# A fixed, searched instruction order for a fused convolution-and-attention kernel, with the convolution kernel's transform moved into attention

## The chip, the cores and the metric

The kernel runs on one core of one Trainium2 chip. The metric is the device time of one execution in microseconds (us), median of several runs. A profile of one execution shows when each engine worked: PE (matmul; PEld its weight loads), DVE (the vector engine), ACT (the scalar engine), POOL (the general engine) and SP (which issues transfers), with the DMA queues beside them.

## The reference

Two results are blended by a gate that comes from the input. S is 2048, D is 640; everything is bfloat16.

```python
g = sigmoid((A_q * gate_w).sum(-1, keepdims=True))
# A: a short causal convolution over k (4 taps), times v, then a long causal
# convolution over all 2048 positions, one kernel per channel
k_shift = sum(k_pad[:, t:t+S, :] * shift_k[:, 3-t] for t in range(4))
kv = k_shift * v
y = irfft(rfft(pad(kv)) * rfft(pad(ssm_k)))[:, :S] + kv * ssm_D
a = q * y                                    # q is A_q
# B: 32 heads of 20, each position sees itself and 7 earlier ones, two apart
qh, kh, vh = split(A_q @ wqkv)
b = softmax(qh . kh[idx] * scale) . vh[idx]  @ wo
out = g * a + (1 - g) * b
```

## The kernel before

**Attention.** Positions are split by parity, so that the distance of two becomes one, and cut into 18 blocks of up to 114 queries and 121 keys. The steps, by the names of their tiles:

- `xpose` (tile `tx` to `xT`): the input comes in eight pieces (`xn`) and is transposed on PE.
- `vproj` (`psv` to `VW`): V for all heads, 18 units of ten matmuls of 320 columns. `VW` holds 21 columns a head: 20 of V and a column of ones, which gives the softmax denominator.
- `qkproj` (`pj` to `stg`): q and k for 128 of 640 columns at a time (`ft` 0 to 4), 30 units of ten matmuls, copied to staging tiles.
- `fragger`: POOL issues a DMA for each head's fragment from `stg` to one of three pairs of buffers `qb`, `kb`. These hold mask rows too, written once by POOL (`masks`).
- `score_gen` (`sc` to `ETall`): per set of four heads, 72 score matmuls and ten exponentials on ACT into a ring of eight buffers (`NET`).
- `pv_gen` (`O` to `oS`): 72 matmuls of 21 columns a set, then on DVE a reciprocal and a multiplication with it into `oS`, in two parts (48 and 24 matmuls).
- `op_tr` and `outproj` (`tr` to `oT`, `op` to `bl`): 90 transposes of the result, then the output projection in 16 tiles, each evacuated by ACT with the factor 1-g.

**Long convolution.** A two-stage transform (stage 1, `s1_unit`: 8 matmuls a unit, 20 units; stage 2, `s2_unit`: 12 matmuls, 22 units) is applied to the convolution kernel (`h_stream`) and to kv (`u_stream`), each in two parts P = 0 and 1. Its results are multiplied with each other on DVE (`products`), where the kernel's transform is needed also with its two halves swapped: `swaps` copies it by eight DMAs of 640 KB from the tiles `SX` and `Hs` to `Hw`. Then come the inverse's first stage (`inverse1`, 320 matmuls, tile `i` to `UC`) and second stage (`final`, 512 small matmuls, `yb`), and in `final` DVE multiplies with q, adds `bl`, and SP stores groups of up to three of the 16 tiles. `conv` computes the four taps on DVE, 42 operations, `conv_v` the product with v.

**What sets the order.** Each step is a generator that asks for an engine, with what it depends on. A planner (class `Plan`) keeps a cost model of the engines, the four PSUM slots and the DMA lanes, and grants at each step the request that could start first, shifted by hand-set priorities (`PRI`). What it decides is a fixed order of instructions on each engine; on the chip each engine works through its list in that order. Three choices in memory matter here: `oS` has a place of its own, the constants `G` of stage 2 and the transform of part 0 (`SX`) lie where the convolution's inputs (`KX`) were, so `load_G` and the stage 1 of the kernel's transform start only after `conv` and `vproj` are done.

```python
def load_G():
    yield Req("S", 1.0, [ev("conv"), ev("grow"), ev("vproj")])
    SX = p0.tile([128, 10240 + 8192], BF, name="SX", tag="KX")
```

Of the kernel before, what the change touches and what calls it, by code (L numbers as in the profile page):

```python
# [39 lines left out]
NET = 8  # L40
# [7 lines left out]
WARM = 8  # L48
BG = 1266.0
# [59 lines left out]
INF = float("inf")  # L109


class Ev:
    __slots__ = ("t", "eng")

    def __init__(self, t=None, eng="X"):
        self.t = t
        self.eng = eng


class Bank:  # L120
    __slots__ = ("free",)

    def __init__(self):
        self.free = Ev(0.0)
# [6 lines left out]
class Req:  # L131


    def __init__(self, engs, cost=0.0, deps=(), take=0, give=(), n=0, move=0.0, pri=None, mode=None, bg=None, mm=0, lean=0.0):
        self.engs, self.cost, self.deps, self.take, self.give, self.n, self.move = engs, cost, deps, take, give, n, move
        self.pri, self.mode, self.bg, self.mm, self.lean = pri, mode, bg, mm, lean


LAT = {("P", "A"): 230.0, ("P", "D"): 230.0, ("A", "P"): 120.0, ("D", "P"): 120.0, ("A", "D"): 100.0, ("D", "A"): 100.0}
SWITCH = 110.0  # L140
LEAN_QK = -248.0
LEAN_V = 87.0
LEAN_H = -137.0
PRI = dict(loads=0, fragger=0, xpose=-9.2, score_gen=-8.6, pv_gen=-5.7, conv=-1.6, conv_v=-24.1, bulk=0, conv_end=0, qkproj=-4.2, vproj=-4.8,
           gate=-0.8, load_G=0, h_slot=0, p2_slot=10.2, u_slot=0, swaps=0, load_T=0, op_tr=4.7, outproj=37.5, load_q=0, products=6.3, final=-18.6,
           h_stream=(-3.7, -4.9), u_stream=(0.9, 2.5), inverse1=(33.7, 30.7))
PAGE = 256
FETCH = 3600.0


class Plan:


    def __init__(self, nslots):
        self.at = dict(P=0.0, A=0.0, D=0.0, G=0.0, S=0.0, Q=0.0)
        self.mode = None
        self.count = 0
        self.page = 0.0
        self.pipe = 2000.0
        self.row = 0.0  # L160
        lane = []
        self.lane = {"S": lane, "Q": lane, "G": []}
        self.slots = [Bank() for _ in range(nslots)]
        self.streams = []
        self.log = []

    def add(self, gen, pri):
        self.streams.append([pri, gen, next(gen)])

    def cost(self, r, e):  # L170
        if r.n:
            return 160.0 + 0.84 * r.n if e == "A" else 140.0 + 1.03 * r.n
        return r.cost[e] if isinstance(r.cost, dict) else r.cost

    def start(self, r, e):
        t = self.at[e]
        if e == "P" and r.mode != self.mode:
            t += SWITCH
        for d in r.deps:
            if d.t is None:  # L180
                return INF
            t = max(t, d.t + LAT.get((d.eng, e), 60.0))
        if r.take:
            free = sorted(s.free.t + 120.0 if s.free.t is not None else INF for s in self.slots)
            t = max(t, free[r.take - 1])
        if r.move and len(self.lane[e]) >= 8:
            t = max(t, self.lane[e][-8])
        if r.bg is not None:
            t = max(t, self.pipe - r.bg)
        return t  # L190

    def best(self, r):
        found = []
        for e in r.engs:
            s = self.start(r, e)
            found.append((s + self.cost(r, e) + (r.lean if e == "A" else 0.0), s, e))
        end, s, e = min(found)
        return s + self.cost(r, e) if s < INF else INF, s, e

    def run(self):  # L200
        while self.streams:
            pick = None
            for k, (pri, gen, r) in enumerate(self.streams):
                end, st, e = self.best(r)
                if st == INF:
                    continue
                p = pri if r.pri is None else r.pri
                key = (st + 120.0 * p, p, k)
                if pick is None or key < pick[0]:
                    pick = (key, k, st, end, e)  # L210
            assert pick is not None, [(s[1].__name__, s[2].engs) for s in self.streams]
            _, k, st, end, e = pick
            pri, gen, r = self.streams[k]
            g = Grant()
            g.eng, g.banks = e, []
            if e == "P":
                c = self.count + 2 * r.mm
                while self.count // PAGE < c // PAGE:
                    into = (self.count // PAGE + 1) * PAGE - self.count
                    x = max(st, self.page) + (end - st) * into / max(1, 2 * r.mm)  # L220
                    late = max(0.0, self.page + FETCH - (st + (end - st) * into / max(1, 2 * r.mm)))
                    st, end = st + late, end + late
                    self.page = st + (end - st) * into / max(1, 2 * r.mm)
                    self.count += into
                    r.mm -= into // 2
                    st = self.page
                    end = max(end, st)
# [724 lines left out]
```

## Time and profile before

| | |
|---|---|
| Median of three runs | 251.53 us (249.74, 251.53, 256.14) |
| The profiled execution | span 246.1 us from its first to its last instruction; its own run time is not listed apart, so what lies around the span is taken as 3.6 us (to the lowest run) to 5.4 us (to the median) |
| PE / DVE / ACT / POOL busy | 215.8 / 185.8 / 168.6 / 68.8 us |
| First score | 42.75 us |
| Last normalization of attention | ends at 139.9 us |
| First inverse stage starts | 197.6 us |
| Second inverse stage starts | 220.9 us |

The busy time of PE in this profile counts a matmul from its start to its modelled end, so two in a row overlap; the distance of two starts is the better price. "Granted clock" is the share of full speed that PE was allowed. A row of the view by stretches reads: stretch, its length, then for PE, PEld, DVE, ACT and POOL the busy us and (x) the number of instructions, then the granted clock, the busy share of the DMA engines, and GB/s. A row of the view by groups reads: line, engine, operation, output<-input, shapes, xcount, then busy us and mean ns of one, then idle time before them and what ended it. A row of the view in order of time reads: start, length, engine, line, operation, [idle before it <- what ended that].

### The profile page before, as it was taken

To read this page: it belongs to the slowest core of one execution; us is meant where nothing else is said; L and a number is where in the kernel's file an instruction comes from. 1 tells how busy PE (TensorE), PEld (TensorE's weight loads), DVE (VectorE), ACT (ScalarE), POOL (GpSimd) and SP (SyncE) were. 2 spreads that over 40 slices of the span, in tenths; PEclk is the share of its full clock that TensorE was granted. 3 is DMA by queue.
4 is the path that set the end of the run, shared out by engine and by line. 5 is a ranking of instruction groups with operands and counts; after the bars stand their busy time and mean duration, and the time that the engine had idled before them with its cause. 6 is when DMAs were issued, how large, how long until landed. Compare 5 with 4: busy or idle time off the path is not lost.

```text
span 246.1 us, 8342 instructions
## 1 busy us (share of the span) xinstructions
PE 215.8 (88%) x3654; PEld 167.2 (68%) x3654; DVE 185.8 (76%) x220; ACT 168.6 (69%) x222; POOL 68.8 (28%) x147
## 2 busy tenths in 40 slices
PE   6799999899796999999999999896979999984590
PEld 2699887776464667565766788785867799983350
DVE  1424499999879999978788899995899993134942
ACT  2143543774478785789889799988375589768871
POOL 6699699106719144619000000000000000000000
PEclk9999999999999799995555599999799999999568
DMA  6999965898994959698910000699939910400754
GB/s 230 305 348 192 177 81 137 148 158 142 180 146 95 150 96 138 122 164 245 257 67 4 3 4 3 151 221 212 218 61 204 268 20 3 109 0 5 179 147 107
DMA packets 59580, 33.83 MB, mean 137 GB/s; under 512 B 49212, under 2 KB 56008, under 8 KB 58904
## 3 DMA queue, kind: packets, MB, share of 16 engines
q1 hardware_dynamic: 55192, 27.08, 55.0%
q0 software_dynamic: 3792, 5.81, 10.5%
q8 instruction: 28, 0.46, 0.9%
q10 hardware_dynamic: 560, 0.42, 0.5%
q14 instruction: 8, 0.07, 0.1%
HBM read 20.01 MB, written 2.62 MB: 92 GB/s over the span
## 4 chain that ended last, share of the span: by engine, by line
PE 49%; DMA 13%; POOL 13%; issue 9%; ACT 9%; DVE 4%; SPq 1%; ACTq 0%; POOLq 0%; DVEq 0%
PE op L854 10%; PE pj L575 9%; PE i L820 7%; PE O L664 6%; DMA Hw<-SX 5%; PE sc L636 5%; ACT ETall L643 4%; PE s L713 4%; DMA kb<-stg 3%; POOL qb L614 3%; DMA mm<-ca_mm 3%; DMA KX<-in_A_k_dram 3%; PE psv L528 2%; POOL kb L427 2%; POOL qb L428 2%
## 5 line engine op out<-in xcount | busy, mean ns | idle before, releaser
L643 ACT ACTIVATE ETall<-sc 121x912 bf16<-121x912 f32 (+1 forms) x80 | 63.4, 855 | 12.5 <-PE sc L636 11.6
L575 PE MATMUL pj<-xT,Wqk 128*128 128x342 bf16 (+1 forms) x300 | 49.0, 314 | 1.0 <-ACT ETall L643 0.6
L575 PEld LDWEIGHTS <-Wqk 128*128 128x128 bf16 x300 | 28.4, 98 | 15.8 <-issue 1.4
L481 DVE TENSOR_TENSOR KX<-KX 128x1760 bf16<-128x1760 bf16 (+1 forms) x24 | 27.6, 1161 | 4.3 <-issue 4.0
L614 POOL DMA_DIRECT2D qb<-stg x36 | 18.1, 505 | 36.8 <-PE sc L636 14.6
L528 PE MATMUL psv<-KX,xT 128*121 128x320 bf16 x180 | 27.3, 300 | 1.0 <-DVE xT L286 1.0
L636 PE MATMUL sc<-qb,kb 31*128 31x114 bf16 x576 | 23.4, 241 | 5.4 <-ACT ETall L643 2.0
L284 ACT CAST UC<-s 128x960 bf16<-128x960 f32 (+2 forms) x25 | 22.3, 971 | 7.9 <-PE s L713 6.7
L854 PE MATMUL op<-wo,oT 128*128 128x512 bf16 (+1 forms) x160 | 25.7, 322 | 0.0
L528 PEld LDWEIGHTS <-xT 128*121 128x121 bf16 x180 | 23.4, 134 | 2.2 <-issue 1.2
L713 PEld LDWEIGHTS <-SX 64*128 64x128 bf16 x512 | 19.5, 96 | 7.8 <-issue 7.0
L636 PEld LDWEIGHTS <-kb 31*128 31x128 bf16 x576 | 13.7, 104 | 15.1 <-issue 9.3
L284 ACT CAST stg<-pj 128x684 bf16<-128x684 f32 (+1 forms) x17 | 12.5, 746 | 14.9 <-PE pj L575 9.2
L284 ACT CAST VW<-psv 121x640 bf16<-121x640 f32 x15 | 10.4, 696 | 17.8 <-PE psv L528 17.8
L854 PEld LDWEIGHTS <-oT 128*128 128x128 bf16 x160 | 17.1, 150 | 7.4 <-issue 2.3
L286 DVE CAST UC<-s 128x1024 bf16<-128x1024 f32 (+1 forms) x17 | 19.5, 1195 | 0.0
L488 DVE TENSOR_TENSOR KX<-KX 128x1760 bf16<-128x1760 bf16 (+1 forms) x18 | 18.8, 1042 | 0.3
L614 POOL DMA_DIRECT2D kb<-stg x36 | 17.9, 505 | 3.4 <-ACT stg L284 2.9
L858 ACT ACTIVATE bl<-op,omg 128x640 bf16<-128x640 f32 x16 | 12.7, 794 | 8.6 <-PE op L854 8.6
L820 PE MATMUL i<-F,Hw 128*128 128x128 bf16 x160 | 18.3, 219 | 0.0
L286 DVE COPY xT<-tx 128x1280 bf16<-128x1280 bf16 x8 | 6.5, 824 | 15.6 <-PE tx L467 15.6
L664 PEld LDWEIGHTS <-ETall 121*128 121x128 bf16 x576 | 16.5, 100 | 2.5 <-issue 1.7
(73 smaller groups left out, 376.4 us busy)
## 6 DMA issues: line engine op xcount, KB each, us to landing
xn<-in_A_q_dram SPq DMA_DIRECT2D x8, 320.0 KB, 8.0
KX<-in_A_k_dram SPq DMA_DIRECT2D x8, 320.0 KB, 11.8
vin<-in_A_v_dram SPq DMA_DIRECT2D x8, 320.0 KB, 7.1
h_lin<-in_A_ssm_k_dram SPq DMA_DIRECT2D x16, 160.0 KB, 4.9
Hw<-SX SPq DMA_DIRECT2D x4, 640.0 KB, 7.8
Hw<-Hs SPq DMA_DIRECT2D x4, 640.0 KB, 11.9
out_dram<-SX SPq DMA_DIRECT2D x20, 120.0 KB, 2.2
kb<-stg POOLq DMA_DIRECT2D x28, 85.1 KB, 3.6
```

Source lines behind the costliest of these rows:

```text
L284: nc.scalar.copy(dst, src)
L286: nc.vector.tensor_copy(dst, src)
L481: eng.tensor_tensor(d, kin[:, n + 3 - j:n + 3 - j + m, :], w.to_broadcast([128, m, QC]), ALU.mult)
L528: nc.tensor.matmul(ps[0:BK, n0 // 320, 0:320], lhsT=xT[:, dt, s0:s0 + BK], rhs=Wv[:, dt, n0:n1], start=(dt == 0), stop=(dt == NDT - 1))
L575: nc.tensor.matmul(ps[:, i, 0:n], lhsT=Wqk[:, dt, w, 128 * ft:128 * ft + 128], rhs=xT[:, dt, s0:s0 + n], start=(dt == 0), stop=(dt == NDT ...
L614: nc.gpsimd.dma_start(dst[r0:r0 + rows, 0:wd], stg[fa - f0:fb - f0, 0:wd])
L636: nc.tensor.matmul(sc[:, hh, BQ * bb:BQ * bb + BQ], lhsT=kb[r:r + DH + NF, BK * b:BK * b + 128], rhs=qb[r:r + DH + NF, BQ * b:BQ * b + BQ] ...
L643: nc.scalar.activation(ETall[0:BK, e, :, 0:BQ * nb], sc[0:BK, :, 0:BQ * nb], ACT.Exp, scale=SCALE)
L664: nc.tensor.matmul(O[:, (b - b0) // 6, c0:c0 + 21], lhsT=ETall[0:BK, e, hh, BQ * bb:BQ * bb + 128], rhs=VW[0:BK, b, 4 * t + h4, :], start= ...
L713: nc.tensor.matmul(ps[:, c, 160 * jj:160 * jj + 160], lhsT=st["G"][rows, j0 + jj, rr, :], rhs=Am[rows, rr].rearrange("p o (q j) l -> p j ( ...
L820: nc.tensor.matmul(d, lhsT=st[(key, P)][:, c, o + il // 4, :, il % 4], rhs=M[:, k, :], start=(k == 0), stop=(k == 1), skip_group_check=True)
L854: nc.tensor.matmul(op[:, n0:n1], lhsT=oT[:, ft].rearrange("p h m a -> p a (h m)")[:, t, :], rhs=wo[:, ft, n0:n1], start=(ft == 0), stop=(f ...
```

## The change

The planner is gone. The order of all requests now stands in the program as a string of 846 letters (`ORDER`), one for each request, with a `-` where the second of two possible engines is taken; a small class (`Steps`) grants them in that order. Apart from that:

- Head: the eight pieces of the input come first on SP, the weights for `ft` 0 and half of V come on ACT's queue after the constants, k comes last row first in three pieces, then its halo. The memsets of `ETall` and `VW` move from POOL to DVE. Twelve warm-up matmuls in place of eight.
- First heads first: `ft` 0 of q and k alternate, and their fragments too; V is projected by halves of the heads (`vproj0`, `vproj1`), the second half during attention.
- `oS` becomes a view of `VW`: the normalized output of a set is written over columns of V that were used up. The tiles `G`, `H0` (transform of part 0, in the place of `xn`) and both `Hw` now have places that come free early, and `h_lin` holds one part at a time.
- The convolution kernel's transform runs from the middle of attention on: all of stage 1, and 16 of the 22 units of stage 2, stand ahead of the last attention matmul. The addition of `ssm_D` moves from POOL to DVE.
- An O matmul takes up to three heads' columns (63, 63, 42, 21); what it writes beyond its own head is overwritten by the next ones. Seven `ETall` buffers in place of eight.
- q is loaded in two halves of eight tiles (`load_q0`, `load_q1`) and multiplied with g on DVE, tile by tile; the second inverse's evacuation is a plain copy, and takes all tiles of a group at once. The groups of the tail are (0,3), (3,3), (6,2), (8,3), (11,3), (14,2).

```diff
-NET = 8
+NET = 7
-WARM = 8
+WARM = 12
+TAIL = [(0, 3), (3, 3), (6, 2), (8, 3), (11, 3), (14, 2)]
...
-class Plan:
+class Steps:
+    def run(self, order):
+        for word in order.split():
+            other = 0
+            for c in word:
+                if c == "-":
+                    other = 1
+                    continue
+                k = STREAMS.index(c)
+                self.grant(k, self.streams[k][1].engs[other])
...
+    G = p0.tile([128, 32, 2, 128], BF, name="G", tag="G")
+    h_lin = p0.tile([128, PL, 2, 64], BF, name="h_lin", tag="HL")
+    xn = p0.tile([128, 8, 2, D], BF, name="xn", tag="H0")
+    VW = p0.tile([128, NB, H, DH + 1], BF, name="VW", tag="VW")
+    oS = VW[:].rearrange("p b h e -> p b (h e)")
...
     def pv_gen():
-  nc.tensor.matmul(O[:, (b - b0) // 6, c0:c0 + 21], lhsT=ETall[0:BK, e, hh, BQ * bb:BQ * bb + 128],
-                   rhs=VW[0:BK, b, 4 * t + h4, :], start=True, stop=True, skip_group_check=True)
+  nh = min(3, 4 - h4)
+  nc.tensor.matmul(O[:, (b - b0) // 6, c0:c0 + 21 * nh], lhsT=ETall[0:BK, e, hh, BQ * bb:BQ * bb + 128],
+                   rhs=VW[0:BK, b, 4 * t + h4:4 * t + h4 + nh, :].rearrange("p h e -> p (h e)"),
+                   start=True, stop=True, skip_group_check=True)
...
-    def load_q():
-        for n, (a, b) in enumerate(((4, 16), (0, 4))):
...
+    def load_q(half):
+        yield Req("N", 0.0, [ev(f"{k}s2{P}") for k in "hu" for P in range(2)] if half else [ev("hs10"), ev("hs11")])
+        q = p0.tile([128, 8, D], BF, name=f"q{half}", tag="G" if half else "HL")
+        for g in range(4):
+            r = yield Req("S", 600.0, move=1400.0)
+            nc.sync.dma_start(q[32 * g:32 * g + 32], ...)
+        for t in range(8):
+            r = yield Req("D", 235.0, [Ev(r.done.src), ev("gate")] if t == 0 else [])
+            nc.vector.tensor_scalar(q[:, t], q[:, t], g_nat[:, 8 * half + t:8 * half + t + 1], None, ALU.mult)
...
     def final():
-  nc.scalar.activation(yb[:, tt, 320 * k:320 * k + 320].rearrange("p (q c) -> p q c", q=2),
-                       pss[k][:, :, 160 * tt:160 * tt + 160], ACT.Copy, scale=g_nat[:, t0 + tt:t0 + tt + 1])
+  copy(r.eng, yb[:, 0:m, 320 * k:320 * k + 320].rearrange("p t (q c) -> p q t c", q=2),
+       pss[k][:, :, 0:160 * m].rearrange("p q (t c) -> p q t c", c=160))
```

In the built order SP's list ends: four loads of `q0`, eight swap copies, four stores of the first group, one load of `q1`, four stores, two loads of `q1`, four stores, the last load of `q1`, twelve stores.

577 lines of the change are left out of this document (250 added, 327 removed).

## The prediction

> **What bounds the kernel now.** I read the page first, then the busy time of each engine in the stretches between the phases, then the groups of instructions, and last the order in time where one phase hands over to the next.
>
> ```profile
> span 246.1 us, 8342 instructions
> PE 215.8 (88%) x3654; PEld 167.2 (68%) x3654; DVE 185.8 (76%) x220; ACT 168.6 (69%) x222; POOL 68.8 (28%) x147
> ...
> 0.00:34.00 34.00, 30.55 (x247) 25.00 (x248) 13.39 (x13) 11.89 (x16) 27.12 (x42) 1.00 1.07 240
> 43.70:138.70 95.00, 87.54 (x1540) 61.24 (x1542) 84.21 (x105) 72.40 (x93) 32.35 (x86) 0.84 0.77 136
> 138.70:183.50 44.80, 38.87 (x811) 33.93 (x809) 40.87 (x41) 35.85 (x42) 0.00 (x0) 0.92 0.56 119
> 183.50:197.60 14.10, 14.10 (x102) 10.40 (x102) 14.10 (x27) 8.52 (x11) 0.00 (x0) 1.00 0.96 214
> 197.60:220.90 23.30, 22.21 (x352) 21.05 (x351) 11.35 (x18) 19.41 (x21) 0.00 (x0) 1.00 0.13 31
> 220.90:246.10 25.20, 13.14 (x542) 8.35 (x541) 12.48 (x12) 16.10 (x35) 0.00 (x0) 0.77 0.41 107
> 112.00:140.00 28.00, 25.88 (x566) 19.20 (x562) 23.50 (x31) 24.24 (x32) 4.34 (x12) 0.50 0.41 107
> ```
>
> No engine is full over the whole span, but one is in each stretch. To 43.7 us PE loads and projects. Attention (43.7 to 138.7; DVE ends its last normalization at 139.9) keeps PE busy for 87.5 of 95.0 us, DVE for 84.2 and ACT for only 72.4. From there to 197.6 DVE sets the pace (54.9 of 58.9 us): copies out of PSUM, then the products. The first inverse stage takes 23.3 us and is full of PE. In the last 25.2 us nothing is full: a chain through all engines and the output stores. The last row is the second fact that matters: from 112 to 140 us the granted clock is 0.50 although PE shows 25.9 of 28.0 us busy.
>
> **Prices.** Busy time over count, so that overlapping starts are taken out.
>
> ```profile
> L643 ACT ACTIVATE ETall<-sc 121x912 bf16<-121x912 f32 x48 | 41.7, 931 | 6.3 <-PE sc L636 5.8
> L643 ACT ACTIVATE ETall<-sc 121x684 bf16<-121x684 f32 x32 | 22.1, 740 | 6.3 <-PE sc L636 5.8
> L284 ACT CAST stg<-pj 128x726 bf16<-128x726 f32 x7 | 5.4, 768 | 5.4 <-PE pj L575 5.4
> L284 ACT CAST VW<-psv 121x640 bf16<-121x640 f32 x15 | 10.4, 696 | 17.8 <-PE psv L528 17.8
> L284 ACT CAST UC<-i 128x1024 bf16<-128x1024 f32 x17 | 16.2, 1020 | 2.7 <-PE i L820 2.2
> L284 ACT CAST UC<-s 128x960 bf16<-128x960 f32 x15 | 13.6, 968 | 5.8 <-PE s L713 4.6 <-ACT UC L284 1.0
> L858 ACT ACTIVATE bl<-op,omg 128x640 bf16<-128x640 f32 x16 | 12.7, 794 | 8.6 <-PE op L854 8.6
> L488 DVE TENSOR_TENSOR KX<-KX 128x1760 bf16<-128x1760 bf16 x15 | 16.1, 1070 | 0.3
> L676 DVE TENSOR_TENSOR oS<-O,rd 114x480 bf16<-114x480 f32 x24 | 15.0, 654 | 0.6
> L673 DVE RECIPROCAL rd<-O 114x48 f32<-114x48 f32 x8 | 3.6, 454 | 2.5 <-PE O L664 2.5
> L286 DVE CAST UC<-s 128x1024 bf16<-128x1024 f32 x12 | 13.8, 1213 | 0.0
> L286 DVE CAST UC<-s 128x960 bf16<-128x960 f32 x5 | 5.7, 1152 | 0.0
> L751 DVE TENSOR_TENSOR Hw<-UC,Hw 128x960 bf16<-128x960 bf16 x20 | 12.9, 647 | 0.0
> L713 PE MATMUL s<-UC,SX 64*128 64x160 bf16 x256 | 12.2, 237 | 4.0 <-DVE oT L286 1.9 <-issue 1.4 <-ACT UC L284 0.5
> L697 PE MATMUL s<-F,h_lin 64*128 64x128 bf16 x160 | 11.8, 291 | 1.0 <-ACT ETall L643 0.8
> ```
>
> **Head of the kernel.** POOL's constants, PE's order and the first conv taps:
>
> ```profile
> 1.84 3.59 PE L438 MATMUL wu<-KX 128*128 128x512 bf16 x8 [1.84 <-DVE KX L435]
> 27.04 1.61 PE L575 MATMUL pj<-xT,Wqk 128*128 128x342 bf16 x10
> 28.49 1.52 PE L528 MATMUL psv<-KX,xT 128*121 128x320 bf16 x10
> 29.84 1.65 PE L575 MATMUL pj<-xT,Wqk 128*128 128x349 bf16 x10
> 42.75 0.67 PE L636 MATMUL sc<-qb,kb 31*128 31x114 bf16 x8
> ...
> 36.23 3.50 POOL L614 DMA_DIRECT2D qb<-stg  x7 [0.19 <-issue]
> 28.27 4.91 DVE L481 TENSOR_TENSOR KX<-KX 128x1760 bf16<-128x1760 bf16 x2 [3.98 <-issue]
> ```
>
> Ten psv matmuls take 29.84-28.49 = 1.35 us, ten pj 28.49-27.04 = 1.45 us. Today PE runs 8 warm-up (3.6), 80 transposes (about 4.5), 140 psv (18.9) and 80 pj (11.6) ahead of the first score: 38.6 us from 1.84 on, and the score starts at 42.75, so 2.3 us are lost. Afterwards it is 12 warm-up (12x0.45 = 5.4), 80 transposes, 90 psv (12.2) and 60 pj (8.7): 30.8 us, first score at 1.84+30.8+2.3 = 34.9. POOL does not hold it up: its first fragment leaves at 36.23 today behind three mask pairs, 16 small instructions, eight halo DMAs and the memsets of ETall and VW; halo DMAs go to SP, the memsets to DVE (which stands idle there), the constant mm is fetched ahead of the weights. POOL is free at about 22 us, the eight fragment DMAs of set 0 take 8x0.5 us, and land near 31. The extra 1.8 us of warm-up lie before the last x block and are counted. But 50 psv (6.8 us) and 20 pj (2.9 us) are only moved behind the first score: the start is 7.9 us earlier and owes PE 9.7.
>
> The conv taps need the first k rows, on SP behind 5.2 MB; at the 240 GB/s of the first row of stretches 5.7 MB arrive at 23.8 us. The two first taps took 4.91 us beside POOL's mask copies; now those are over, and I price all 42 at the L488 row.
>
> **Attention.** It takes in 188 of 256 s2 matmuls of the conv-kernel transform with 16 of 22 copies, all its stage 1, and the 9.7 us. Counted from the built order, from the first score to the last normalization:
> - ACT: 80 exponentials 41.7+22.1 = 63.8; 18 stg copies x0.77 = 13.9; 9 VW x0.69 = 6.2; 8 transform copies, half at 0.95 and half at 0.91, 7.5; the gate 0.7. Sum 92.1 (today 72.4).
> - DVE, from 23.8: 42 taps 35x1.07+7x0.9 = 43.8; normalization 24x0.63 and 16 reciprocals, half of them shorter than the row, 6 together, 21.1; 27 transform copies at about 1.15 = 31; 6 stg 5.2; the four v products 6.2; small ones 1. Sum 108.3, so not before 132.1.
> - PE: 90 psv 12.2, 240 pj 34.8, 188 s2 at 0.048 and 160 s1 at 0.074 at most (its row is mostly from half clock) 20.8, the gate 1.3; scores and O below. Sum at most 98.
>
> ```profile
> 51.98 1.38 PE L664 MATMUL O<-VW,ETall 121*128 121x21 bf16 x48
> 121.41 0.58 PE L636 MATMUL sc<-qb,kb 31*128 31x114 bf16 x16
> ...
> 139.36 0.66 DVE L676 TENSOR_TENSOR oS<-O,rd 114x480 bf16<-114x480 f32 x1
> ```
>
> The O row prices PE's 576 O matmuls at 28 ns with 21 columns, 16.2 us; 576 scores are some 12.6 at full clock, and by the row from 121.41 (16 in 0.58 us) 1.7 times that at half. Widened to as many as 63 columns they stream 63x0.42 ns = 27 ns (0.42 is 1.35 us over ten times 320 columns), under the 28: nothing at full clock. At 0.50 it would be 53 ns, at most 0.9 us more a set on average. That is the bound. I take zero: the row of 0.50 lies where projections had run out, and here they are spread over sets 0 to 5. If the clock falls in sets 6 and 7 alone, PE's 12 us there become some 21 against 16 of ACT: up to 5 us, in the range. [...]
>
> So three engines have 92 to 100 us of work in about 100. ACT is last: 34.9+0.6 to start, 92.1, about 6 us in set 0 in which PE works through 70 pj and 50 psv (17 us) while ACT has 13, and 1.7 for the last O and its normalization: 135.3 if nothing else is lost. The same sum at today's occupancy (72.4/95.0 = 76%) is 34.9+0.6+92.1/0.76+1.7 = 158. Today's ACT was underfed, not obstructed, so I go near the low end: 4.2 us lost, T0 = 139.5, range 135 to 150. Seven ET buffers in place of eight can cost one exponential a set (0 to 7 us); it is inside that range. Attention's end thus stays where it is (139.9); the gain must come behind it.
>
> **Behind attention.** DVE sets the pace: 3 H copies 3.1, 7 u stage-1 copies 8.1, 5 u stage-2 copies 5.4, 5 oT 6.0, gate 0.6, 8 q products (no such row; the 640-element sum at 240.99 below takes 0.49, a quarter of that is the least that I can see, I take 0.3) 2.4, then 28 products x0.645 = 18.1 before the inverse of part 1 may start: 43.7; with 5% loss T0+46. Beside it ACT has 13 copies of 1024, 17 of 960 and 11 op outputs (12.4+15.5+8.7 = 37 us), and PE 324 s2 (15.6), 160 s1 (8 to 12), 90 transposes (5) and 110 op matmuls (15.5; the row of 183.50 has 102 matmuls in 14.10 us): 44 to 48. PE just fits; if not, up to 3 us, in the range.
>
> ```profile
> 170.68 0.66 DVE L751 TENSOR_TENSOR SX<-UC,SX 128x960 bf16<-128x960 bf16 x1 [2.73 <-DMA Hw<-SX]
> ```
>
> Today DVE also waits 2.73 us here for the swaps. They no longer wait for attention's buffers, but still for the last copy (T0+4); 8x0.64 MB at the 214 GB/s of the stretch rows are 24.5 us, T0+30.5, when DVE asks for part 1's at T0+30: covered, 0 to 2 us. Today this way takes 197.6-139.9 = 57.7. Saved: 11.7.
>
> First inverse: 20 copies on ACT alone, 20x0.95+2 = 21.3 against 23.3; the rest of the products (16x0.645 = 10.3) end beside part 1. Saved 2.0. The second inverse starts at 139.5+46+21.3 = 206.8.
>
> **The tail**, where the change costs:
>
> ```profile
> 224.36 1.28 PE L893 MATMUL i<-UC,T 32*32 32x160 bf16 x120 [1.78 <-issue]
> 233.14 5.16 PE L854 MATMUL op<-wo,oT 128*128 128x512 bf16 x20
> ...
> 226.99 16.99 SPq L911 DMA_DIRECT2D out_dram<-SX  x24
> 240.99 0.49 DVE L908 TENSOR_TENSOR SX<-SX,bl 128x640 bf16<-128x640 bf16 x1 [0.28 <-ACT bl L858]
> SX<-in_A_q_dram SPq DMA_DIRECT2D x4, 160.0 KB, 3.4
> ```
>
> ACT's evacuation gets cheaper (two copies of 960 for six scaled ones), but the second half of q is loaded by SP between the stores: the fourth of its DMAs stands behind the stores of the third group, and DVE's q products for tiles 8 to 15 stand ahead of its last three groups. By today's pattern the third group's sum ends 12 us in: two groups with the 1.78 us PE stall, 20 op matmuls (1.41 us each ten at full clock, 2.58 in the row at 233.14), the small group. Then four stores at 0.6 us (4 issues from 241.5 to 244.0), the load 0.5+3.4, eight q products 2.4, three groups 2x2.4+1.7, and today's 4.6 us from the last sum to the end: 12+2.4+3.9+2.4+6.5+4.6 = 31.8 against 25.2. Lost 6.6. Without that wait PE ends near 20, and the tail is 26.5.
>
> **Sum**: 206.8+31.8 = 238.6 against 246.1, that is -0.4 -11.7 -2.0 +6.6 = -7.5. The median of the runs lies 5.4 above the profiled span (251.53), the lowest 3.6; with 5.4: 244.0 us, 3% less. About 2% is what a measurement of this kernel can tell from no change.
>
> **Rivals.**
> 1. The q load does not bite, because DVE reaches it late anyway: 238.6-5.3 = 233.3, so 238.7. Against it: the order in SP's queue is fixed. Chance 0.14.
> 2. The moved transform is paid back in attention: part of its 16 copies (16 us over two engines) prolong it to T0 = 147, span 246.1, 251.5: no change. For it: three engines above 90%. Chance 0.22.
> 3. Slower: ACT, fed in a fixed order by a PE that is itself full, stays at 76% as today. T0 = 158, span 257.1, so 262.5 us. It decides from an occupancy of about 80% down (T0 above 152). Against it: today's low share is largely lack of work. Chance 0.14.
> 4. The clock halves from set 4 on: there PE has 50 pj, 288 scores and O, 80 s1 and 176 s2, some 32 us at full clock and, at the 1.7 of the score row, 55 or more at half, against 39 for ACT, T0 near 156: 260. Against it: sets with 20 to 40 pj kept 1.00 today. Chance 0.04.
>
> The forecast has the remaining 0.46, 239 to 249 by itself. Faster by over 2%: 0.14, most of the forecast and a little of rival 2, 0.56; slower: 3 and most of 4, 0.16; between them 0.28. The range leaves out rivals 3 and 4 and the luckiest ends: 234 to 256.
>
> **What would show it.** First score near 35 us; last normalization near 139.5 (135 and 147 decide between forecast and rival 2) with ACT above 90% between; granted clock 1.00 there (rival 4); first inverse 46 us later; a DVE wait of 5 to 6 us for the q DMA before its last three groups (rival 1: none). I am wrong if the last normalization comes after 150 or that wait is missing.

## The result, and the profile after

The changed kernel takes 275.67 us (median of six runs, 271.55 to 282.04) beside 250.98 us for the kernel before (247.16 to 256.14). The ratio is 1.094, 95% interval 1.080 to 1.108: slower by 9%, where 3% faster was predicted. Below, the time of a kernel is the mean of its undisturbed runs (273.4 us for the changed one, five in two series; 249 to 251 for the one before), since some runs of each kernel are some per cent longer, among them the profiled ones of pe_light, filler, late_part1, quiet_late, late_pe_light and changed_again, whose rows serve for places and shares rather than times. The runs counted for one kernel, two to seven of them, lie up to 4.3 us apart, so a difference of under 3 us between two kernels says little by itself.

First the page of the changed kernel, then its stretches: the phases, and attention cut at the last O of each set (sets 3 and 4 in three pieces).

```profile
span 269.5 us, 8335 instructions
PE 224.4 (83%) x3658; PEld 171.2 (64%) x3658; DVE 178.3 (66%) x227; ACT 176.6 (66%) x217; POOL 54.3 (20%) x126
```

```profile
36.10:64.40 28.30, 25.00 (x277) 17.87 (x278) 18.59 (x19) 17.68 (x24) 9.02 (x26) 0.94 1.06 161
64.40:81.40 17.00, 17.00 (x244) 12.22 (x246) 13.84 (x17) 13.12 (x19) 2.11 (x5) 1.00 1.11 158
81.40:95.80 14.40, 13.64 (x236) 9.26 (x236) 12.02 (x15) 9.83 (x14) 6.56 (x22) 1.00 0.62 117
...
105.40:119.10 13.70, 9.02 (x188) 6.91 (x188) 8.29 (x11) 10.29 (x14) 4.47 (x9) 1.00 1.18 170
119.10:131.40 12.30, 10.94 (x190) 7.35 (x192) 6.58 (x7) 7.82 (x11) 3.50 (x7) 0.80 0.27 74
131.40:145.10 13.70, 12.36 (x214) 8.05 (x212) 9.60 (x11) 9.33 (x13) 3.45 (x7) 0.81 0.19 46
145.10:155.50 10.40, 8.48 (x207) 6.67 (x208) 8.00 (x10) 8.59 (x11) 0.00 (x0) 0.91 0.80 185
155.50:168.00 12.50, 11.45 (x236) 9.39 (x235) 9.39 (x13) 7.55 (x10) 0.00 (x0) 0.66 0.12 21
168.00:217.40 49.40, 43.30 (x658) 35.57 (x653) 41.43 (x61) 36.57 (x43) 0.00 (x0) 0.93 0.51 108
...
236.80:269.50 32.70, 14.70 (x562) 10.14 (x561) 14.75 (x20) 13.52 (x17) 0.00 (x0) 0.79 0.48 122
36.10:168.00 131.90, 117.40 (x1889) 83.56 (x1889) 93.87 (x110) 92.05 (x119) 31.63 (x80) 0.91 0.74 122
```

Against the rows of the prediction the span falls apart like this (us):

| | before | forecast | after |
|---|---|---|---|
| to the first score | 42.8 | 34.9 | 36.1 |
| attention, to the last normalization | 97.2 | 104.6 | 131.7 |
| from there to the first inverse | 57.7 | 46.0 | 49.6 |
| first inverse | 23.3 | 21.3 | 19.4 |
| the rest | 25.2 | 31.8 | 32.7 |
| span | 246.1 | 238.6 | 269.5 |

Four of the five are within 4 us. Attention is off by 27 of the 31 us. ACT is busy there for 92.05 us, as the forecast's sum has it (92.1), yet only 70% of the time. PE is busy for 117.4 where the sum had 98 at most. The rows by set show four kinds of trouble: in set 0 (36.1 to 64.4) PE is busy for 25.0 of 28.3 us; from 64.4 to 95.8 at full clock it has hardly a pause; at 119 us there is a hole (9.02 of 13.7); from 119 on the clock is 0.66 to 0.91.

**What PE's work cost.** Groups of instructions in attention (count | busy us, mean ns | idle us ahead of them), the scores of the kernel before in its own attention, and a piece of the changed kernel in order of time:

```profile
L508 PE MATMUL pj<-xT,Wqk 128*128 128x342 bf16 (+1 forms) x240 | 43.6, 333 | 1.0 <-ACT ETall L586 0.9
L579 PE MATMUL sc<-qb,kb 31*128 31x114 bf16 x576 | 26.9, 225 | 7.1 <-DMA kb<-stg 3.1 <-ACT ETall L586 2.1 <-ACT H L222 0.8
L609 PE MATMUL O<-VW,ETall 121*128 121x63 bf16 (+2 forms) x576 | 19.8, 190 | 1.9 <-ACT ETall L586 0.9 <-issue 0.8 <-DVE SX L224 0.2
```

```profile
L636 PE MATMUL sc<-qb,kb 31*128 31x114 bf16 x576 | 23.4, 241 | 5.4 <-ACT ETall L643 2.0 <-DMA kb<-stg 2.0 <-DVE oS L676 1.1
```

```profile
66.14 0.38 PE L579 MATMUL sc<-qb,kb 31*128 31x114 bf16 x8
66.45 1.57 PE L459 MATMUL psv<-WvT,xT 128*121 128x320 bf16 x10
...
78.39 1.67 PE L508 MATMUL pj<-xT,Wqk 128*128 128x349 bf16 x10
79.99 0.40 PE L641 MATMUL s<-F,h_lin 64*128 64x128 bf16 x8
...
119.14 0.64 PE L641 MATMUL s<-F,h_lin 64*128 64x128 bf16 x8 [2.98 <-DVE h_lin L706]
...
120.19 2.96 PE L508 MATMUL pj<-xT,Wqk 128*128 128x342 bf16 x10
123.09 0.40 PE L641 MATMUL s<-F,h_lin 64*128 64x128 bf16 x8
```

A modelled end overlaps the next start, so I add up distances of starts, without the idle time in brackets. From the first score to the last O, 130.7 us, that gives: scores 24.5 (forecast 12.6), projections 41.8 (34.8), O 18.8 (16.2), psv 13.0 (12.2), the transform 17.6 (20.8), the gate 1.2 (1.3). Together 116.8, and 13.9 us of idle time. The same adding for the kernel before, to its last O, gives 88.6 and 7.2: there are 7.1 us more of projections, 7.1 of psv, 8.9 of transform, 5.1 of scores and O, and 6.7 of idle time. Nearly all that was moved in came on top.

Two causes can be seen. The first is the order. At full clock a unit of 8 scores takes 66.45-66.14 = 0.31 us, and a projection behind scores 79.99-78.39 = 1.60; I had priced 16 scores at 0.35 and the projection at 1.45. My price fits the kernel before where its order puts 16 scores side by side, 46.54-46.20 = 0.34 us:

```profile
46.20 0.40 PE L636 MATMUL sc<-qb,kb 31*128 31x114 bf16 x16
46.54 1.57 PE L528 MATMUL psv<-KX,xT 128*121 128x320 bf16 x10
```

Its group row, 23.4 us for 576 scores, is longer for more than one reason: busy times overlap, and 215 of these scores ran at half clock. The 361 at full clock come to 11.1 us from start to start, 0.49 for 16.

The second cause is the clock: behind the hole at 119 ten projection matmuls take 2.90 us (120.19 to 123.09), at half clock. Sorted by the granted clock, 31 of the changed kernel's 240 projection matmuls ran at half clock, 291 ns each, and 209 at full clock, 157 ns each. So of the 7.0 us by which projections exceed the forecast some 4 are the clock; of the scores' 12 only about 1 is.

**The tail** went as forecast: DVE waits 6.54 us for the fourth of q1's DMAs, which stands behind twelve stores.

```profile
249.77 1.78 SPq L849 DMA_DIRECT2D out_dram<-q  x4
251.59 1.28 SPq L809 DMA_DIRECT2D q<-in_A_q_dram  x1
...
256.28 2.46 DVE L812 TENSOR_SCALAR q<-q,g_nat 128x640 bf16<-128x640 bf16 x8 [6.54 <-DMA q<-in_A_q_dram]
```

### The profile page after: what moved, and what is told of

It reads as the page before. It is cut to its first block, busy times and chain, and to the rows that moved or that the text cites. A ratio compares the mean times of both kernels' runs of the same rounds, so it can differ in the third digit from the quotient of the medians.

```text
span 269.5 us, 8335 instructions
## 1 busy us (share of the span) xinstructions
PE 224.4 (83%) x3658; PEld 171.2 (64%) x3658; DVE 178.3 (66%) x227; ACT 176.6 (66%) x217; POOL 54.3 (20%) x126
## 4 chain that ended last, share of the span: by engine, by line
PE 57%; DMA 15%; ACT 11%; DVE 8%; issue 4%; SPq 2%; POOL 1%; ACTq 0%; DVEq 0%
PE pj L508 16%; PE op L793 8%; PE O L609 6%; PE s L657 6%; ACT UC L222 6%; PE psv L459 5%; PE sc L579 5%; PE i L759 4%; ACT ETall L586 4%; DMA h_lin<-in_A_ssm_k_dram 3%; PE s L641 3%; DMA WvT<-in_B_wqkv_dram 3%; DMA kb<-stg 3%; DMA qb<-stg 3%; DMA q<-in_A_q_dram 2%
## 5 line engine op out<-in xcount | busy, mean ns | idle before, releaser
L508 PE MATMUL pj<-xT,Wqk 128*128 128x342 bf16 (+1 forms) x300 | 52.8, 328 | 1.0 <-ACT ETall L586 0.9
L222 ACT CAST UC<-s 128x960 bf16<-128x960 f32 (+2 forms) x30 | 27.4, 995 | 9.4 <-PE s L657 8.1
L222 ACT CAST stg<-pj 128x684 bf16<-128x684 f32 (+1 forms) x24 | 18.0, 752 | 23.1 <-PE pj L508 16.1
L579 PE MATMUL sc<-qb,kb 31*128 31x114 bf16 x576 | 26.9, 225 | 7.1 <-DMA kb<-stg 3.1
L224 DVE CAST SX<-s 128x1024 bf16<-128x1024 f32 (+1 forms) x20 | 23.3, 1186 | 9.8 <-PE s L641 8.9
L459 PE MATMUL psv<-WvT,xT 128*121 128x320 bf16 x180 | 26.0, 300 | 3.0 <-DMA WvT<-in_B_wqkv_dram 3.0
L579 PEld LDWEIGHTS <-kb 31*128 31x128 bf16 x576 | 15.5, 99 | 18.5 <-issue 10.8
L657 PEld LDWEIGHTS <-G 64*128 64x128 bf16 x512 | 19.8, 99 | 7.4 <-issue 5.6
L609 PE MATMUL O<-VW,ETall 121*128 121x63 bf16 (+2 forms) x576 | 19.8, 190 | 1.9 <-ACT ETall L586 0.9
L222 ACT CAST UC<-i 128x1024 bf16<-128x1024 f32 x20 | 18.4, 1124 | 0.1
L844 DVE TENSOR_TENSOR q<-yb,q 128x1920 bf16<-128x1920 bf16 (+1 forms) x6 | 6.3, 1043 | 18.0 <-ACT yb L222 18.0
```

The lines of the kernel that those rows point to most:

```text
L222: nc.scalar.copy(dst, src)
L224: nc.vector.tensor_copy(dst, src)
L459: nc.tensor.matmul(ps[0:BK, par, 0:320], lhsT=xT[:, dt, s0:s0 + BK], rhs=Wv[:, dt, 320 * hp:320 * hp + 320], start=(dt == 0), stop=(dt == ...
L508: nc.tensor.matmul(ps[:, i, 0:n], lhsT=Wqk[:, dt, w, 128 * ft:128 * ft + 128], rhs=xT[:, dt, s0:s0 + n], start=(dt == 0), stop=(dt == NDT ...
L579: nc.tensor.matmul(sc[:, hh, BQ * bb:BQ * bb + BQ], lhsT=kb[r:r + DH + NF, BK * b:BK * b + 128], rhs=qb[r:r + DH + NF, BQ * b:BQ * b + BQ] ...
L609: nc.tensor.matmul(O[:, (b - b0) // 6, c0:c0 + 21 * nh], lhsT=ETall[0:BK, e, hh, BQ * bb:BQ * bb + 128], rhs=VW[0:BK, b, 4 * t + h4:4 * t ...
```

## The experiments

The leading theory was that PE sets attention's end, because the split order makes its work dearer than its streaming time. The rivals: late data (set 0's fragments, h_lin's second load) with the fall of the clock behind them, and ACT in its fixed order, as in the prediction's third rival. All edits are to the changed kernel, except in prices and before_wide.

### The prices alone

> Not the kernel: matmuls alone, of its shapes, on 128 rows of the input, nothing on ACT or DVE; the output is the input. Sections, each at full clock as far as it goes: projections of ten matmuls with 342 columns back to back; score units of 8 on one half of the row groups only; score units on alternating halves; a lone score unit between projections; two score units, then two projections; O units of 48 with 21 columns and with up to 63; score units between O units of 24. Theory that the split order costs PE: a lone 8 takes 0.28 to 0.35 us and the projection behind it 1.55 to 1.62, so a score and a projection 1.85 to 1.95; side by side two units take 0.35 to 0.40, and the same work in the paired order 1.60 to 1.72 a pair. O of 48: 1.36 to 1.42 us narrow, 1.40 to 1.50 wide. Rival (the prices of the forecast, and the long times in attention are waits that the records don't show): 8 scores 0.18, projection 1.45, O 1.35 in any order.

```profile
30.20 11.76 PE L98 MATMUL ps<-big 128*128 128x342 bf16 x80
41.89 3.49 PE L100 MATMUL ps<-big 31*128 31x114 bf16 x128
45.32 5.97 PE L102 MATMUL ps<-big 128*128 128x342 bf16 x40
...
51.23 1.85 PE L104 MATMUL ps<-big 31*128 31x114 bf16 x128
53.02 5.97 PE L106 MATMUL ps<-big 128*128 128x342 bf16 x40
58.92 0.38 PE L108 MATMUL ps<-big 31*128 31x114 bf16 x8
59.23 1.62 PE L109 MATMUL ps<-big 128*128 128x342 bf16 x10
60.79 0.38 PE L108 MATMUL ps<-big 31*128 31x114 bf16 x8
...
107.11 7.64 PE L118 MATMUL ps<-big 121*128 121x21 bf16 x288
114.59 7.36 PE L120 MATMUL ps<-big 128*128 128x342 bf16 x40
121.79 8.01 PE L122 MATMUL ps<-big 121*128 121x63 bf16 x288
129.65 5.96 PE L124 MATMUL ps<-big 128*128 128x342 bf16 x40
```

From start to start: ten projection matmuls in a row of its own 11.69/8 = 1.46 us. Eight scores on alternating halves of the row groups 1.79/16 = 0.11, always on the same half 3.43/16 = 0.21, alone between projections 0.31, and the projection behind them 1.56. So a score and a projection by turns cost 1.87 where the parts in rows of their own cost 1.57: 0.30 us more, without any other engine. Two and two cost 1.67 each (from 81.34 to 84.68, 3.34 us for two of each). The theory's prices of scores and projections stand, the rival's fall; the O units were cheaper than either had them (1.25 us narrow and 1.31 wide for 48). Why a lone unit costs 0.31 where rows of them cost 0.11 to 0.21 was not shown; the prices by themselves speak against a finely mixed order.

The last rows belong to the clock, below.

### Which engine: less PE work, less ACT work, the units in pairs

```diff
 # pe_light
-for dt in range(NDT):
+for dt in range(NDT if ft == 0 else 3):
 # act_light
-nc.scalar.activation(ETall[0:BK, e, :, 0:BQ * nb], sc[0:BK, :, 0:BQ * nb], ACT.Exp, scale=SCALE)
+nc.scalar.activation(ETall[0:BK, e, :, 0:BQ * nb // 2], sc[0:BK, :, 0:BQ * nb // 2], ACT.Exp, scale=SCALE)
 # pairs (ORDER, one of 23 places)
-eeyyeeyyeejykeef
+yyeeeeyyjykeeeef
```

> Leaves out 2 of the 5 matmul steps of the projections of ft 1 to 4: 96 matmuls of attention, 14 to 15 us of PE, and nothing on ACT, DVE or in the queues. Theory that PE's work bounds attention: its end moves 9 to 15 us earlier. Rival (ACT's order or late data): under 4 us.

> Exponentials over half of their columns (the buffers are filled once ahead): ACT loses some 28 of its 92 us in attention, PE, DVE and the queues nothing. Theory that PE's work bounds attention: its end moves by 2 to 6 us, which are PE's waits for ETall. Rival (ACT's order bounds it): 12 us or more.

> Only the order is changed: the two score units of a block group, which use two row groups of PE each, always stand next to each other (23 pairs joined; runs of 12, 16 and 28 score matmuls in place of 6, 8, 12, 16, 18 and 28; 111 runs on PE in attention in place of 137). Theory that PE bounds attention and that lone score units and switches cost it: a joined pair takes 0.35 to 0.4 us less, the busy time of scores falls from 26.9 to 17 to 20 us, and attention ends 6 to 10 us earlier. Rival (late data and the clock set the end, PE's busy time only fills the waits): scores get shorter, the end moves by under 2 us. Second rival (ACT, fed in bursts, holds PSUM): slower by 1 to 4 us.

pe_light takes 270.3 us: 3 less for 14 us of PE. act_light takes 272.9: nothing for 26 us of ACT.

```profile
38.50:168.60 130.10, 114.14 (x1853) 80.11 (x1854) 90.44 (x106) 66.23 (x118) 31.63 (x80) 0.92 0.69 121
```

ACT is busy for 66.23 us in attention instead of 92.05, and it lasts 130.1 us from first score to last O, where the changed kernel's two profiles have 130.7 and 135.5. That ends the third rival: ACT's order is not the bound. But pe_light missed the leading theory's 9 to 15 us as well. PE's work does set the pace of sets 1 to 3, where PE has hardly a pause: they take 46.2 us in the changed kernel (64.4 to 110.6), 45.0 in act_light, and 42.3 in pe_light, although its clock was 0.95 and 0.87 in two of them. In the same profile its set 0 gave most of that back, at clock 0.75, with 31.6 us in place of 28.3. And pairs, which made scores cheaper as forecast (busy 22.0 us in place of 26.9), was slower by 12: 285.4 us. PE's waits in its attention:

```profile
PE O L609 <- ACT ETall L586: 5.8, 7, 1.1
PE pj L508 <- ACT stg L222: 4.3, 3, 3.2
```

O waits for the last exponential of its group seven times, projections for the place that ACT's copy has to free. Is it ACT's pace? pairs_act_light joins the two edits.

> The paired order together with exponentials over half of their columns, which alone changed nothing. Theory that pairing lost because ACT, given two exponentials at a time, holds PE's four places in PSUM and answers too late: with short exponentials the paired order is no longer slower, 266 to 274 us, and PE's waits for ETall fall from 17 to under 6 us. Rival (pairing loses through late projections and fragments): 280 to 286 us.

278.7 us, between the two forecasts: 6.8 less than pairs, where short exponentials alone gave 0.4. So about half of what pairing lost comes from ACT answering two exponentials at a time too late for PE's four places in PSUM; the other half, 5.8 us over act_light, was not placed. The fine order has a price on PE and hides the way through ACT; in the one paired order that was run, the first did not go without the second.

### Late data: h_lin's second load and set 0

```diff
 # h_once
-yield Req("N", 0.0, [ev("hs10")])
-yield from load_h(1)
 # h_after_set0: only the order, letters "a" behind set 0's "d"
 # quiet_set0: that order, and k's rows 0 to 49 left out
-for q in range(4):
+for q in range(4 if k == 0 else 0):
     nc.sync.dma_start(kin[32 * q:32 * q + 32, 3 + n0:3 + n1, :], ...)
```

> The second load of h_lin (eight DMAs) and its D addition are left out; part 1 of the transform reads part 0's data, so every PE, ACT and DVE step but that addition stays. Theory that PE's own work bounds attention: only the 3.0 us of PE's wait at 119 us go, at most 4 us of the last normalization at 167.8. Rival (late data set attention's end, and the clock drops that follow them): the wait and the half clock from 120 to 145 us both go, 7 to 12 us.

> The first load of h_lin, 1.28 MB, and the first of G start behind set 0's eight fragment DMAs and no longer ahead of them; nothing else is moved. Theory that PE's work bounds attention: set 0's waits of PE (3.1 us for kb) shrink, 2 to 4 us off the 28.3 us of set 0, and as much off the whole. Rival (late data set the pace): 5 to 8 us off set 0. If the pieces of k and not h_lin crowd the queues: under 1 us.

> Leaves out the load of k's rows 0 to 49 (zeros in their place), 2.05 MB, and puts h_lin's first load and the first of G behind set 0's fragment DMAs: next to nothing else is in the queues while set 0's fragments travel. Theory that set 0 is late for its data: it shrinks from 28 to 32 us to 20 to 23 us, no wait for kb or qb stays and the clock is 1.00 from 40 to 48 us; the whole gains 6 to 9 us. Rival (set 0 is full of PE work, 25 us of it): 1 to 3 us.

```profile
117.30:132.80 15.50, 13.25 (x270) 9.47 (x269) 9.80 (x11) 13.78 (x18) 5.26 (x11) 1.00 0.45 125
...
146.10:157.40 11.30, 10.51 (x206) 8.03 (x208) 8.24 (x10) 8.19 (x11) 0.00 (x0) 0.68 0.83 186
157.40:168.00 10.60, 9.55 (x200) 7.49 (x202) 8.30 (x11) 7.60 (x10) 0.00 (x0) 0.70 0.05 9
```

```profile
36.00:60.30 24.30, 22.92 (x275) 17.16 (x276) 18.20 (x19) 17.64 (x24) 6.99 (x14) 1.00 1.07 191
106.50:125.50 19.00, 12.82 (x211) 8.56 (x212) 7.62 (x8) 11.23 (x14) 3.34 (x7) 0.91 0.75 118
```

h_once takes 270.9 us, 2.5 less, as the leading theory has it and far from the rival's 7 to 12. Set 4 falls from 20.8 us (110.6 to 131.4) to 15.5 at clock 1.00 (first row), but the clock falls later instead, to 0.68 and 0.70 in sets 6 and 7. h_after_set0 takes 277.0, 3.6 more, with 31.0 us for set 0: so it was not h_lin's load that crowded set 0. quiet_set0 shrinks set 0 from 28.3 to 24.3 us at clock 1.00, with no wait for a fragment left. The whole is 6.2 us below h_after_set0, whose order it has, and only 2.6 below the changed kernel (270.8): PE then stands still for longer at 112 to 117, 5.1 us in front of h_lin (12.82 busy of 19.0 us).

### Limits in series

late_part1 changes only the order. It relieves two places at once.

```diff
 # late_part1 (ORDER)
-fffhqzzzzzzz-zddddddddeddddddeejjeejm0eej-00eejdddeej-00eejfeeeeeedddd-00feeeef
+fffhzzzzzzz-zddddddddeddddddeejjeejzeej-zzeejdddeej-zzeejfeeeeeedddd-zm0feeeef
 ...
-ffzzz-zzzz-zzzz-z112-2222
+ffzzz-zzz0-0000-0112-2222
 # and, as in q1_first
-555uuuuuuuuuttttwuuuuuwwttuuuuttwwwwwwwwwuu
+555wwwwuuuuuuuuuttttuuuuuttuuuuttwwwwwwwwuu
```

> The four DMAs of q's second half stand ahead of all stores in SP's queue; nothing else is changed. Tail theory: the 6.5 us that DVE waits for that q at about 255 us go away, and the stretch from the first inverse's end falls from 32.7 to 26 to 27.5 us; the whole kernel gains 5 to 6.5 us against the changed kernel. Rival: DVE and the stores are late anyway (PE's output projections set the pace), and the stretch falls by less than 2 us.

> The order with q1's loads ahead of the stores, once more. Tail theory: the stretch behind the first inverse was 26 us where it had been 32.7, so the whole is 5 to 6.5 us below the changed kernel of the same series. Rival (attention ended 5 us later for a reason that the order brings): 1 to 3 us.

> The changed kernel itself once more, beside the two that follow, because gains of 2 to 5 us are to be read against it. Every theory: 271 to 276 us, the last O 130 to 132 us after the first score; if a start at 38 us in place of 36.1, as most of its variants showed, is its usual one, the last O comes at 168 to 173 rather than at 166.8.

> Only the order: three units of the transform's part 0 that stood behind attention take the place of part 1's first three, whose last three go behind instead, so that h_lin's second load has some 6 us more; the load of T goes behind that of wo and q; q1's loads go ahead of the stores. Theory of sums (each place has its own limit, and relieving two of them adds up): set 4 falls from 21 to 15 to 17 us, the tail from 32.7 to 26 to 27, the whole gains 8 to 12 us against the changed kernel, so 262 to 266, still slower than before. Rival (the wait for h_lin comes back at another place or the clock takes it): the tail's 4 to 6 us alone.

> The quiet queues of set 0 (k's rows 0 to 49 left out, h_lin's first load behind set 0's fragments) together with the order that gives h_lin's second load more time and puts q1 ahead of the stores. Theory that each place has its own limit and that set 0's gain was lost in the wait for h_lin: set 0 some 24 us, and the whole 5 to 8 us below the order alone, 254 to 259. Rival (what set 0 gives comes back later whatever the order, through the clock or ACT): 260 to 265, as the order alone.

> The order that gives h_lin's second load more time, with 2 of 5 matmul steps of the projections of ft 1 to 4 left out, 14 to 15 us of PE in attention. Theory of limits in series (taking PE work away alone brought little because the wait for h_lin stood behind it): now 6 to 10 us below the order alone, 252 to 257. Rival (the granted clock falls where PE has less to do, and takes it back): under 4 us, and the mean clock in attention falls by 0.03 or more.

```profile
242.10:267.90 25.80, 14.68 (x562) 10.18 (x561) 14.67 (x20) 13.58 (x18) 0.00 (x0) 0.85 0.41 104
```

```profile
114.20:130.40 16.20, 14.12 (x282) 10.06 (x281) 10.24 (x12) 13.99 (x19) 5.25 (x11) 0.98 0.53 84
```

q1 ahead of the stores shortens the rest from 32.7 to 25.8 us, and no wait for q is left: for the tail itself the theory holds. Of these 6.9 the whole shows only 3.4 (270.0 us, seven runs in two series; 4.4 within the second) where 5 to 6.5 were expected: in both its profiles and in that of changed_again attention took 135.3 to 135.5 us, so the 130.7 of the changed kernel's profile is at the low end of what this order takes. changed_again itself takes 273.9 us (both series together 273.4), with its first score at 38.4. late_part1 takes 261.9 us, 11.5 less than the changed kernel: set 4 takes 16.2 us and the theory of sums holds. It is even more than h_once and q1_first gave one by one (2.5 and 3.4). Of the kernels that leave nothing out it is the fastest, and at 1.046 (1.035 to 1.057) still slower than the kernel before.

On top of it, quiet_late brings another 3.3 us (258.6; 5 to 8 expected, none by the rival) and late_pe_light 4.7 (257.2; 6 to 10, or under 4); by the ratios to the kernel before in their own series (1.046, 1.036 and 1.032) it is 2.6 and 3.4. With two or three runs counted for each, these gains are hardly clear of the spread. quiet_late does keep its short set 0 (25.1 us). late_pe_light comes out nearer to its rival, and the rival's sign is there: the mean clock of the runs counted is 0.89 to 0.91, late_part1's 0.92 and 0.94. As an estimate, 0.03 of 257 us are up to 8 of the 14 us of PE work that were taken away. So the limits stand in series, as late_part1 shows, and by that estimate the clock takes a part of a gain back.

### The clock

```diff
 # filler
-nc.tensor.matmul(O[...], ...)
+for _ in range(1 + (t > 3)):
+    nc.tensor.matmul(O[...], ...)
 # narrow_o; before_wide does the reverse in the kernel before
-nh = min(3, 4 - h4)
+nh = 1
```

> Issues each O matmul of sets 4 to 7 twice into the same place: 288 matmuls, 9 us of PE at full clock, and nothing else. Theory that sets 4 to 7 lose to the clock, which halves behind stretches where PE is underused: with more to do the half-clock stretches from 120 to 163 us shrink from 19 to under 10 us and attention ends at most 4 us later. Rival (the clock has its own times, or PE's work alone sets the end): attention ends 8 to 12 us later.

> O matmuls back to 21 columns each, nothing else. By the prices measured alone (48 in 1.25 us narrow, 1.31 wide) PE gets 0.1 us a set back: no change beyond 1 us. Rival (the wider form costs the clock or the queue behind it more): 3 us or more faster.

> The kernel before, with O matmuls of up to 63 columns and nothing else; the order of instructions is the same. By the prices measured alone PE pays 0.06 us per 48 more, 0.8 us in all. Theory that wider matmuls keep the clock up (21 columns in the changed kernel: clock 0.88 and 5 to 7 us more): the granted clock from 112 to 140 us rises above 0.6, and the whole gains 1 to 4 us. Rival (the clock there follows from PE having too little to do, which 0.1 us a set does not change): 0.50 as before, the time within 1 us or up to 3 us longer, since at half clock 63 columns take longer than 21.

filler takes 280.2 us, 7 more for 8 us of extra PE work (288 matmuls at the 27 ns that the prices give), with clocks of 0.93 and 0.95 in the runs counted (0.90 to 0.93 without): the clock rises, but by less than the work costs. That is over the first theory's 4 us and just short of the rival's 8 to 12.

The last rows of the prices bear on the clock, in the one execution that was profiled. Six O units of 48 take 7.48 us narrow and 7.86 wide, each in one row without a pause. But 40 projection matmuls behind the narrow ones take 7.20 us, behind the wide ones 5.89:

```profile
107.10:114.50 7.40, 7.40 (x287) 7.39 (x285) 0.00 (x0) 0.74 0.02 4
114.60:121.70 7.10, 7.10 (x46) 4.39 (x43) 0.00 (x0) 0.80 0.00 0
121.80:129.60 7.80, 7.80 (x288) 7.80 (x286) 0.00 (x0) 1.00 0.02 4
```

With 21 columns the clock fell to 0.74 over the stretch while PE was busy all the time; with up to 63 it stayed 1.00. narrow_o agrees in the clock: its mean is 0.88, with 0.50 in its last two sets (0.91 and 0.66 in the changed kernel's rows):

```profile
151.20:163.00 11.80, 11.04 (x208) 8.18 (x208) 8.26 (x10) 8.22 (x11) 0.00 (x0) 0.50 0.81 182
163.00:174.00 11.00, 10.12 (x201) 7.74 (x202) 8.34 (x11) 7.19 (x10) 0.00 (x0) 0.50 0.01 3
```

Its time, 280.2 us, is 6.8 more, but that can't be put down to O. Its sets 5 to 7 take 36.7 us, as the changed kernel's do (36.6), and from first score to last O it takes 134.2, within the 130.7 to 135.5 of the changed order. Its first score comes at 39.7 in place of 36.1 us, ahead of any O matmul, because PE waited 4.7 us for V's first weights in place of 3.0. before_wide is 0.7% slower (0.1 to 1.3%). Its clock from 112 to 140 us is 0.61, which is just over the 0.6 that the theory asked for, but only because the half clock came later: it is 0.50 from 118 to 149 us, as long as in the kernel before (111 to 142). There, where scores and exponentials alternate and PE has no projections, wider O matmuls did not help, and the rival holds.

### The moved transform

transform_behind puts every letter z and 0 of ORDER, h_lin's second load and the first half of q's behind the last f:

```diff
+fff z-zz-zz-zz-zz-zz-zzzzzzzzzaaaaaaaaaaaaaaaazzzzzzzzz-zzzz-zzzz-zzzz-zm0-00-00 ... -000vvvv112
```

> Only the order is changed: all of the conv-kernel transform, with its second load of h_lin and the first half of q's load, stands behind the last attention matmul. Theory that PE's own work bounds attention: its 21 us of stages 1 and 2 and the 3 us wait go, so the last O moves from 166.8 to 140 to 147 us; the stretch behind it grows from 49 to 64 to 72 us because PE had 43 busy there already, and the whole comes out 0 to 12 us faster than the changed kernel: the transform is paid for once in either place. Rival (ACT in its fixed order bounds attention): only ACT's 8 copies, 7.5 us, go, and the last O comes at 157 to 161.

```profile
36.30:149.10 112.80, 100.02 (x1504) 70.11 (x1503) 60.82 (x79) 82.58 (x109) 31.25 (x72) 0.86 0.67 119
132.00:149.10 17.10, 13.88 (x303) 11.35 (x298) 5.29 (x10) 14.58 (x19) 0.00 (x0) 0.50 0.20 61
149.10:241.20 92.10, 66.67 (x1029) 54.93 (x1032) 72.61 (x90) 45.43 (x52) 0.51 (x8) 0.77 0.46 87
```

From first score to last O it is 112.8 us, 18 to 23 less than the changed kernel's 130.7 to 135.5, for 17.6 us of transform and the wait for h_lin: PE's work, as the leading theory has it, not ACT's 7.5 us of copies. But the stretch behind it takes 92.1 us in place of 49.4, not 64 to 72, and the whole 293.7. That is no fair price, as the copies keep their engines and mostly one engine copies at a time: in this order moving the transform back makes the kernel 20 us slower, but whether the move pays against a good order behind attention is not shown. The second row is worth a look: sets 6 and 7 alone, without the transform, run at clock 0.50 and still take only 8 us each, which ACT's work nearly fills (14.58 us busy in the row). With a stage-2 unit between their scores they take 10.4 and 12.5.

## Why the prediction was wrong

- **The failed step** is the sentence "three engines have 92 to 100 us of work in about 100. ACT is last". ACT's sum was right to 0.1 us. PE's "at most 98" was 116.8, and PE came last. The term that was mis-sized most is scores, 12.6 forecast and 24.5 measured; then projections, 34.8 and 41.8. I took the first from 16 scores side by side and the second from rows without scores; the built order splits and alternates them, and the prices show the difference, 0.30 us a pair of units. The group row of the kernel before could have warned me (23.4 us for its scores), though part of that is half clock. Half clock is in the 116.8 too, in most of what the projections have over their forecast: 0.91 over 131.9 us means, as an estimate, some 24 us at half speed, up to 12 us lost. How attention's 27 us divide between the order, the clock and the waits is not settled, since taking 14 us of PE work away gave only 3 to 5.
- **Losses of 4.2 us** were 13.9 us of idle time on PE. The largest pieces: 3.1 us for set 0's kb, 3.0 us for h_lin. The second load was not in my sum at all; I had only counted what the transform computes, not that its second half can't be loaded before the first is used up.
- **The clock.** "I take zero" for the wider O held for its price (0.06 us per 48). Rival 4 had the fall of the clock and mostly the place, from set 4 on, with too small a chance: the clock halved at 119, 130 and 154 us, and at 41 us in set 0, though not throughout. What I held against it, that sets with 20 to 40 pj had kept 1.00, was misread: in the kernel before the clock was 0.50 from 81 to 84 us too, in set 2 with its 20. The 5 us that I kept in the range for sets 6 and 7 came true in size (22.9 us against 16), but not by the clock alone: at half clock without the transform these sets take some 16 us in transform_behind. And I read the row of 112 to 140 in the kernel before, 92% busy at clock 0.50, as a full PE. Its busy time is long because the clock is half (16 scores took 0.58 us there), so the row doesn't show that PE had no room; and the half clock behind idle times of only 0.45 and 0.25 us (ahead of 110.7 and 111.3), which the trace does show, I set aside as a matter of projections that had run out.
- **The rivals.** Rival 3, 262.5 us, came nearest, for a wrong reason: ACT's occupancy fell to 70%, but act_light shows that ACT wasn't the bound. Rival 2 happened, through PE and in full: the moved transform was paid for in attention with 17.6 us of PE, where I had put 7.5 us of copies.
- **Right**: the first score (34.9 and 36.1, though 38.4 in changed_again; PE's wait for V's first weights, 3.0 and 3.7 us, was not in the sum), 46 us behind attention (49.6; the products, the swaps and PE as forecast), the first inverse, and the tail with its wait of "5 to 6 us", 6.5 measured, worth the difference between 31.8 and 26.5 as q1_first shows (32.7 and 25.8).
- **The run's time** lies 2.0 us above the span (271.55 and 269.5), not 5.4, and in later runs of the kernel before it is 1.8. I had set a median against the span of another run; put right, that alone would have made the forecast 3.4 us lower.

What stays open: half of what pairing lost, what narrow O costs, and the 11 us by which late_part1 is still slower than the kernel before. By late_pe_light and quiet_late 3 to 5 us of these may be PE's work or set 0's data; the rest was not separated.

## What to carry to other kernels

Price an engine's work in the order in which it will run, not by runs of one form: a short unit between others costs what its neighbours make of it (eight scores 0.11 us in a row of their own, 0.31 between projections). When three engines are near full, relieving one can show little until the wait behind it is gone too (3 us here for 14 us of PE, nothing for 26 of ACT), so look set by set for which wait ends last, and ask of each smaller buffer which load now has to wait for it. A PE that is busy at half clock is not a full PE (16 scores took 0.58 us there, 0.34 at full clock).

## What the runs showed of the hardware

- The granted clock fell in a row of matmuls without any pause, when each had 21 columns (0.74 over 7.4 us, so about half of them at half clock), and stayed 1.00 over 7.8 us with 21 to 63 columns (47 on average). In both rows the records show PE busy all the time, so that alone did not keep the clock up. As an estimate by the price of 0.42 ns a column, 21 columns stream for 9 of the 26 ns that one takes, 47 for 20 of 27; whether the clock goes by that share was not shown, and the two rows are of one execution.
- In the mixed order the clock halved behind holes of 2.4 us (at 41) and 3.0 us (at 119), and behind holes of under 1 us at a time (at 130 behind 0.87 and 0.30, at 154 behind 0.32 and 0.25). Behind a hole of 0.88 us (at 143) it stayed 1.00, so which idle time halves it was not shown.
- Score units that alternate between the two halves of the row groups took 0.11 us each (a matmul every 14 ns), units on one half 0.21 (every 27 ns).
